# One pool of 13 SBUF buffers for attention's features and the feed-forward tiles, and a new order of the steps

## The chip, the cores and the metric

The kernel runs on one core of one Trainium2 chip. The metric is the time of one execution in device microseconds (us). The engines are TensorE (PE in the profile, its weight loads PEld), VectorE (DVE), ScalarE (ACT), GpSimd (POOL) and SyncE (SP), which issues the DMA transfers here. Each engine takes its instructions in the order in which the program has them, and waits on semaphores for the others.

## What is computed

```python
def phi(x):                                   # q, k: (8, 8, 576, 64), w_phi: (64, 128)
    proj = np.einsum('bhsd,df->bhsf', x, w_phi)
    proj = proj - np.max(np.abs(proj), axis=-1, keepdims=True)
    return np.concatenate([np.exp(proj), np.exp(-proj)], axis=-1)
q_p, k_p = (phi(q), phi(k))
kv = np.einsum('bhsf,bhsd->bhfd', k_p, v)
z = np.sum(k_p, axis=2)
num = np.einsum('bhsf,bhfd->bhsd', q_p, kv)
den = np.einsum('bhsf,bhf->bhs', q_p, z)[..., None] + 1e-06
x = ((num / den).transpose(0, 2, 1, 3)).reshape(4608, 512)
h = x @ w_in                                  # w_in: (512, 1024)
e = np.exp(h - np.max(h, axis=-1, keepdims=True))
solu = h * (e / (np.sum(e, axis=-1, keepdims=True) + 1e-09))
ln = (solu - mean(solu)) / np.sqrt(var(solu) + 1e-06) * g_ln
out = ln @ w_out                              # w_out: (1024, 512)
```

## The kernel before

**Two halves.** Attention is cut into 16 units (8 batches, two groups of four heads each), each with two pairs of heads, called sub 0 and sub 1 here. The feed-forward half is cut into 36 tiles of 128 tokens; nine tiles cover two batches, so a tile can begin when the units of its batches have been divided. The program runs the units and, from the third unit on, the tiles between them.

**A unit.** SP loads q, k and v. PE projects them (`pjq`, `pjk`, and `pjm` for the middle part). DVE takes the maximum and subtracts it (`m`, `dq`, `dk`), ACT takes the exponentials into the features `fq` and `ek`. PE sums keys times values and the keys into `kvT`: the step K (from `ek` and `rawv`), a rest (from `ek` and `vz`) and the step Z, the sum of the keys (from `zacc` and `ones`). DVE turns `kvT` into `kvs` (step kve), one DMA writes it out (`dk<-kvs`, kvo) and a second brings it back in another shape (`kvf<-dk`, kvi). PE then makes `num` and `den` from `fq` and `kvf`; a part of the numerator (step qr) has the output `kvT`. ACT takes `den` to `dn`, DVE inverts it to `cmr`, a DMA writes it (`d<-cmr`), another spreads it over the partitions (`rb<-d`), and POOL multiplies it into the rows of x (`xa`, `xb<-E,rb`).

**A tile.** ACT and POOL split x into a high and a low part (`mxh`, `mxl`). PE makes `h` in 24 matmuls of 512 columns: `win_h` with `mxh`, `win_l` with `mxh`, `win_h` with `mxl`. DVE finds the maximum (`nm`), ACT the exponential (`eu`), DVE the product with h, its statistics (`bst`, `mv`) and a transposed copy (`ub`); two DMAs turn it round (`du<-ub`, `uTs<-du`); ACT and POOL split it again (`uhs`, `uls`), PE makes `o` in 24 matmuls, ACT scales it into `os`, and a DMA writes `out`.

**What sets the order.** The program is a list of 2457 steps. `SEQUENCE` (lines 54 to 184) is a table of their numbers: `order()` (line 229) walks it, and its order is the order of the instructions on every engine. The same walk gives out the SBUF buffers: every tag has a list of free buffers (`SBUF_BUFS`, line 45); a step that needs one takes the first of the list, and a buffer goes back to its end when the last step that reads it has been passed.

**Tags.** `e` has 6 buffers of 4608 bytes per partition, for attention's features `ek` and `fq` and the `eu` of the last tiles. `big` has 8 of 4096 bytes, for the other tiles' `eu`, `ub`, `uTs`, `uhs` and `uls`, and at the start for the weights while they are split.

```python
            for tag, t in o["alloc"]:
                slot[t] = free[tag].pop(0)
            for t in tiles[i]:
                pending[t] -= 1
                if not pending[t]:
                    free[tag_of[t]].append(slot[t])
```

Every instruction is issued through one helper line, so all of them stand under line 260 in the profile, and are told apart by the names of their tiles.

Of the kernel before, what the change touches and what calls it, by code (L numbers as in the profile page):

```python
# [45 lines left out]
    rk=4, rkm=2, rv=3, m=8, d=3, e=6, eh=2, za=2, kf=2, q5=3, pm=1, E=2, dE=2, rb=2, G=1,  # L46
    vz=2, xa=1, xb=1, m2k=5, big=8, nm=2, sm=3, bst=2, mv=2, sa=2, sc=3,
)
SIZES = dict(
    big=4096, e=4608, q5=5120, rk=2048, rv=2048, d=2048, eh=2048, za=2048, m2k=2048, pm=1024, kf=1536, rkm=512, vz=512,  # L50
# [144 lines left out]
def pool(n):  # L195
    return 2.05 * n + 250
# [75 lines left out]
def linear_attention_then_moe(ctx, tc, qT, kT, v, w_phi, w_in, g_ln, w_out, out):  # L272
# [150 lines left out]
    op("warm", "tensor", WARM * 430, -1e4, warm_up, (), (), [("a", "warm")])  # L423
    op("gain", "sync", (475, 450), 5, g_load)
    raw_tag = ("xb", "xa", "xb", "xa")
    w_tag = ("big",) * 8
    w_time = W_TIME
    w_mean_at = W_MEAN
    for i in range(8):
# [877 lines left out]
```

## Time and profile before

| what | us |
|---|---|
| median of 3 runs | 663.02 (662.71 to 663.58) |
| the profiled execution | 664.01 |
| its span, first to last instruction | 662.20 |
| PE busy in the span | 653.7 |
| POOL, DVE, ACT busy | 409.1, 495.1, 368.9 |

The profiled execution has 1.81 us outside its span, and is 0.99 us above the median. TensorE's granted clock is 1.00 in every slice of the span. A row of a timeline begins with its start and its length; several instructions of one kind in a row are put together, with their count behind an x, and the bracket at its end names the time that the engine stood idle before and what ended it.

### The profile page before, as it was taken

The numbers are of one execution on the slowest core, as the hardware profiler recorded it, in microseconds if no ns is written. First come the engines' busy times: TensorE is split into PE (matmuls) and PEld (weight loads), VectorE is DVE, ScalarE is ACT, GpSimd is POOL, SyncE is SP. The second block draws the span as 40 slices with busy tenths as digits, with TensorE's granted clock in tenths as the row PEclk, the third lists the DMA queues.
The fourth block names the chain that finished last, engine by engine and source line by source line (L and its number), as shares of the span: only waits on it lengthen the run. The fifth ranks groups of instructions, "written<-read, shape, count | busy, mean of one in ns | idle before, by whom it ended". The sixth has DMA issues, their size and how long they took to land.

```text
span 662.2 us, 13124 instructions
## 1 busy us (share of the span) xinstructions
PE 653.7 (99%) x4900; PEld 490.5 (74%) x4900; DVE 495.1 (75%) x750; ACT 368.9 (56%) x713; POOL 409.1 (62%) x447
## 2 busy tenths in 40 slices
PE   8999999999999999999999999999999999999997
PEld 6766767668777777777777777877677877788886
DVE  6999987788978687799968879788679665355340
ACT  4997775466564744556565665355745464324221
POOL 0239998757866546667876575856654775455342
PEclk9999999999999999999999999999999999999999
DMA  8987787887487946887667856874786544424241
GB/s 269 346 270 237 221 251 210 270 259 214 134 265 255 296 151 182 272 260 230 201 197 230 287 151 176 266 227 124 229 282 199 191 149 120 123 110 162 112 167 72
DMA packets 133296, 138.45 MB, mean 209 GB/s; under 512 B 55664, under 2 KB 106736, under 8 KB 132720
## 3 DMA queue, kind: packets, MB, share of 16 engines
q1 hardware_dynamic: 133232, 137.61, 65.9%
q8 instruction: 39, 0.64, 0.4%
q14 instruction: 25, 0.20, 0.1%
HBM read 87.10 MB, written 50.48 MB: 208 GB/s over the span
## 4 chain that ended last, share of the span: by engine, by line
PE 87%; DVE 6%; DMA 4%; issue 1%; ACT 1%; SPq 0%; ACTq 0%
PE o L260 30%; PE h L260 29%; PE kvT L260 11%; PE num L260 6%; PE pjk L260 4%; PE pjq L260 4%; PE den L260 2%; DVE m L260 2%; DVE w L260 1%; DVE dq L260 1%; DMA rawq<-in_q 1%; DVE dk L260 1%; DMA pT<-dqd 1%; PE pjm L260 1%; DMA dk<-kvs 1%
## 5 line engine op out<-in xcount | busy, mean ns | idle before, releaser
L260 POOL TENSOR_TENSOR uls<-uTs,uhs 128x1024 fp32r<-128x1024 f32 x36 | 86.6, 2410 | 61.8 <-ACT uhs L260 47.6
L260 PE MATMUL o<-w_out_h,uhs 128*128 128x512 f32 (+1 forms) x296 | 114.6, 387 | 0.0
L260 ACT ACTIVATE ek<-dk 128x512 f32<-128x512 f32 (+1 forms) x160 | 89.7, 584 | 44.1 <-DVE dk L260 39.4
L260 PE MATMUL o<-w_out_l,uhs 128*128 128x512 f32 (+1 forms) x296 | 113.6, 384 | 0.0
L260 PE MATMUL o<-w_out_h,uls 128*128 128x512 f32 (+1 forms) x296 | 113.5, 383 | 0.0
L260 PE MATMUL h<-win_h,mxh 128*128 128x512 f32 x288 | 91.2, 398 | 0.3 <-DVE dq L260 0.3
L260 DVE TENSOR_REDUCE nm<-h 128x1 f32<-128x1024 f32 x36 | 43.9, 1218 | 62.9 <-PE h L260 62.9
L260 PE MATMUL h<-win_l,mxh 128*128 128x512 f32 x288 | 88.9, 390 | 0.0
L260 PE MATMUL h<-win_h,mxl 128*128 128x512 f32 x288 | 88.8, 389 | 0.0
L260 ACT ACTIVATE fq<-pT 128x512 f32<-128x512 f32 (+1 forms) x140 | 74.5, 559 | 21.4 <-DMA pT<-dqd 13.8
L260 POOL TENSOR_TENSOR zt<-ek 128x512 f32<-128x512 f32 x52 | 68.8, 1322 | 24.4 <-ACT ek L260 22.8
L260 ACT ACTIVATE eu<-h,nm 128x1024 f32<-128x1024 f32 x36 | 40.0, 1111 | 69.3 <-DVE nm L260 60.3
L260 PEld LDWEIGHTS o<-w_out_h,uhs 128*128 128x128 f32 x296 | 55.6, 188 | 13.4 <-issue 1.6
L260 PEld LDWEIGHTS o<-w_out_h,uls 128*128 128x128 f32 x296 | 55.6, 188 | 11.0
L260 PEld LDWEIGHTS o<-w_out_l,uhs 128*128 128x128 f32 x296 | 55.6, 188 | 10.6
L260 PEld LDWEIGHTS h<-win_h,mxh 128*128 128x128 f32 x288 | 52.4, 188 | 13.9 <-issue 1.1
L260 PEld LDWEIGHTS h<-win_l,mxh 128*128 128x128 f32 x288 | 54.0, 188 | 11.5
L260 PEld LDWEIGHTS h<-win_h,mxl 128*128 128x128 f32 x288 | 54.1, 188 | 11.5
L260 PE MATMUL kvT<-ek,rawv 128*64 128x256 f32 x512 | 61.9, 384 | 0.0
L260 POOL TENSOR_TENSOR xa<-E,rb 128x576 f32<-128x576 f32 (+1 forms) x32 | 29.7, 931 | 51.9 <-DMA rb<-d 40.7
L260 DVE TENSOR_TENSOR eu<-h,eu 128x1024 f32<-128x1024 f32 x36 | 43.6, 1212 | 17.9 <-ACT eu L260 17.7
L260 PE MATMUL num<-fq,kvf 128*64 128x448 f32 (+1 forms) x304 | 56.2, 500 | 0.0
(96 smaller groups left out, 1231.9 us busy)
## 6 DMA issues: line engine op xcount, KB each, us to landing
du<-ub SPq DMA_DIRECT2D x36, 512.0 KB, 3.7
uTs<-du SPq DMA_DIRECT2D x36, 512.0 KB, 4.9
rb<-d SPq DMA_DIRECT2D x64, 144.0 KB, 4.4
dqd<-dq SPq DMA_DIRECT2D x14, 640.0 KB, 4.3
pT<-dqd SPq DMA_DIRECT2D x14, 640.0 KB, 5.8
out<-os SPq DMA_DIRECT2D x35, 256.0 KB, 3.2
rawq<-in_q SPq DMA_DIRECT2D x32, 256.0 KB, 4.7
rawk<-in_k SPq DMA_DIRECT2D x32, 256.0 KB, 4.5
```

The source lines that it names most:

```text
L260: return self.tc.keep_in_program_order(method(*args, **kwargs))
```

## The change

The tag `big` is gone; `e` has 13 buffers of 4608 bytes, and everything that used `big` takes `e`. That is 59,904 bytes per partition in place of 60,416. The table `SEQUENCE` is a new one in all its 128 lines. No step is added, removed or changed in what it computes.

```diff
-    rk=4, rkm=2, rv=3, m=8, d=3, e=6, eh=2, za=2, kf=2, q5=3, pm=1, E=2, dE=2, rb=2, G=1,
-    vz=2, xa=1, xb=1, m2k=5, big=8, nm=2, sm=3, bst=2, mv=2, sa=2, sc=3,
+    rk=4, rkm=2, rv=3, m=8, d=3, e=13, eh=2, za=2, kf=2, q5=3, pm=1, E=2, dE=2, rb=2, G=1,
+    vz=2, xa=1, xb=1, m2k=5, nm=2, sm=3, bst=2, mv=2, sa=2, sc=3,
...
-    2, 123, 1, 124, 125, 78, 127, 126, 313, 94, 87, 85, 129, 80, 81, 95, 128, 82, 83, 99, 96, 84, 98, 136, 97,
...
+    123, 2, 1, 78, 124, 125, 80, 127, 126, 128, 83, 135, 85, 79, 94, 87, 81, 95, 89, 136, 84, 141, 138, 104, 82,
...
-    w_tag = ("big",) * 8
+    w_tag = ("e",) * 8
...
-        M["uh", t] = sb("big", [P, 8, P], F32R, "uhs")
+        M["uh", t] = sb("e", [P, 8, P], F32R, "uhs")
...
-        M["ul", t] = sb("big", [P, 8, P], F32R, "uls")
+        M["ul", t] = sb("e", [P, 8, P], F32R, "uls")
...
-        e_tag = "e" if tail(t) else "big"
+        e_tag = "e"
...
-            tg = "q5" if t >= TURN_Q else "big"
+            tg = "q5" if t >= TURN_Q else "e"
```

Three places show what the new table does. In the rows, a name stands for the tiles above, and x counts equal instructions in a row.

First, DVE just ahead of the first tile, some 5 us before the first `h`: the subtractions into `dq`, of which the last frees the PSUM bank that `h` takes. Before:

```order
L260 TENSOR_REDUCE m<-pjq 128x4
L260 TENSOR_REDUCE m<-pjk 128x4
L260 STREAM_TRANSPOSE kvs<-kvT 128x3x4x32
L260 TENSOR_TENSOR dq<-pjq,m 128x4x4x32
L260 TENSOR_TENSOR dk<-pjk,m 128x512
L260 TENSOR_TENSOR dk<-pjm,m 128x128
L260 TENSOR_TENSOR dq<-pjq,m 128x4x4x32 x2
```

After:

```order
L260 STREAM_TRANSPOSE kvs<-kvT 128x3x4x32
L260 TENSOR_REDUCE m<-pjq 128x4
L260 TENSOR_REDUCE m<-pjk 128x4
L260 TENSOR_REDUCE m<-pjq 128x4
L260 TENSOR_TENSOR dk<-pjk,m 128x512
L260 TENSOR_TENSOR dq<-pjq,m 128x4x4x32 x2
```

The order among these few is another one, and the same steps stand ahead of the last pair of `dq`, counted from the start of the program: 105 steps with 109 instructions on DVE, 62 steps on PE and 13 on POOL (ahead of the first `mxl`).

Second, PE at the fourth unit's first pair, whose Z (`kvT<-zacc,ones`) stands near the third unit's second `den`. Before:

```order
L260 MATMUL kvT<-ek,rawv 64x256 x8
L260 MATMUL kvT<-fq,kvf 64x128 x4
L260 MATMUL num<-fq,kvf 64x448 x4
L260 MATMUL kvT<-ek,vz 64x256 x4
L260 MATMUL den<-fq,kvf 32x288 x8
L260 MATMUL kvT<-zacc,ones 32x128 x4
L260 MATMUL h<-win_h,mxh 128x512 x2
```

After:

```order
L260 MATMUL kvT<-ek,rawv 64x256 x8
L260 MATMUL num<-fq,kvf 64x448 x4
L260 MATMUL kvT<-fq,kvf 64x128 x4
L260 MATMUL kvT<-ek,vz 64x256 x4
L260 MATMUL kvT<-zacc,ones 32x128 x4
L260 MATMUL den<-fq,kvf 32x288 x8
L260 MATMUL h<-win_h,mxh 128x512 x2
```

Z has moved ahead of the `den`, and on DVE its kve has moved ahead of the turn of tile 2 (`ub<-eu`).

Third, PE at the last `den` of all, that of the sixteenth unit's second pair, for which tile 31 waits. Before, with the first of the 24 matmuls of tile 26's `o` behind it (the `h` of tile 27 and the `o` of tile 28 follow, 24 matmuls each, and then the `h` of tile 31):

```order
L260 MATMUL num<-fq,kvf 64x288 x8
L260 MATMUL num<-fq,kvf 64x448 x4
L260 MATMUL den<-qz,ones 32x288 x4
L260 MATMUL o<-w_out_h,uhs 128x512
L260 MATMUL o<-w_out_l,uhs 128x512
```

After, with the end of tile 28's `o` ahead and the beginning of tile 27's `h` behind (the `o` of tile 26 follows, and then the `h` of tile 31):

```order
L260 MATMUL o<-w_out_l,uhs 128x512
L260 MATMUL o<-w_out_h,uls 128x512
L260 MATMUL den<-qz,ones 32x288 x4
L260 MATMUL num<-fq,kvf 64x288 x8
L260 MATMUL h<-win_h,mxh 128x512 x2
L260 MATMUL h<-win_l,mxh 128x512 x2
```

A `num` has moved from ahead of the `den` to behind it, and the 24 matmuls of one tile's `o` from behind it to ahead of it.

## Rows read from the trace of the kernel before

**Rows 1.** The page, part 1: busy us, share of the span, instructions.
```profile
PE 653.7 (99%) x4900; PEld 490.5 (74%) x4900; DVE 495.1 (75%) x750; ACT 368.9 (56%) x713; POOL 409.1 (62%) x447
```

**Rows 2.** Busy time of each engine in three stretches of the span.
```profile
core 0: us, PE busy (x) PEld busy (x) DVE busy (x) ACT busy (x) POOL busy (x), PEclk, DMA share, GB/s
5.10:67.10 62.00, 59.33 (x824) 42.14 (x823) 61.68 (x110) 50.88 (x98) 26.10 (x16) 1.00 0.89 290
45.40:104.80 59.40, 57.69 (x598) 39.06 (x596) 55.21 (x93) 44.02 (x91) 58.34 (x47) 1.00 0.79 244
...
105.00:655.00 550.00, 550.00 (x3726) 416.31 (x3723) 399.62 (x586) 288.97 (x555) 344.75 (x386) 1.00 0.64 200
```

**Rows 3.** Waits of PE: us in total, times, longest.
```profile
PE kvT L260 <- DMA kvf<-dk: 1.3, 1, 1.3
PE pjm L260 <- DMA rawk<-in_k: 0.9, 2, 0.6
...
PE h L260 <- DVE dq L260: 0.3, 1, 0.3
```

**Rows 4.** Timelines, 0 to 7 and 64 to 70 us: start, length, instruction.
```profile
5.13 1.29 DVE L260 TENSOR_REDUCE m<-pjq 128x4 f32<-128x512 f32 x2 [5.13 <-PE pjq L260]
...
65.68 1.27 DVE L260 TENSOR_TENSOR dq<-pjq,m 128x512 f32<-128x512 f32 x2
...
66.27 1.26 POOL L260 TENSOR_TENSOR mxl<-xa,mxh 128x512 fp32r<-128x512 f32 x1
...
67.10 0.70 PE L260 MATMUL h<-win_h,mxh 128*128 128x512 f32 x2 [0.30 <-DVE dq L260]
...
68.10 0.63 PE L260 MATMUL h<-win_h,mxl 128*128 128x512 f32 x2
```

**Rows 5.** Timeline of PE and of DVE, 87 to 101 us.
```profile
88.00 1.18 PE L260 MATMUL den<-fq,kvf 128*32 128x288 f32 x16
89.00 0.40 PE L260 MATMUL kvT<-zacc,ones 128*32 128x128 f32 x8
...
96.54 1.95 PE L260 MATMUL kvT<-ek,rawv 128*64 128x256 f32 x16
99.79 0.66 PE L260 MATMUL kvT<-fq,kvf 128*64 128x128 f32 x8 [1.31 <-DMA kvf<-dk]
...
89.54 0.58 DVE L260 STREAM_TRANSPOSE kvs<-kvT 128x384 f32<-128x384 f32 x1 [0.73 <-ACT E L260]
```

**Rows 6.** The chain of work that ended last: start, length, step.
```profile
90.15 5.31 DMA dk<-kvs
95.48 4.27 DMA kvf<-dk
...
260.67 1.50 PE num L260 x8
...
266.03 2.95 PE o L260 x12
268.98 2.72 PE h L260 x12
...
561.21 3.59 PE num L260 x24
...
630.93 27.55 PE o L260 x144
```

**Rows 7.** Timeline at the last den, and at the last tile's split.
```profile
564.73 0.69 PE L260 MATMUL den<-qz,ones 128*32 128x288 f32 x8
...
575.80 0.32 POOL L260 TENSOR_TENSOR xa<-E,rb 128x64 f32<-128x64 f32 x1 [5.33 <-DMA rb<-d]
...
577.83 1.12 ACT L260 ACTIVATE eu<-h,nm 128x1024 f32<-128x1024 f32 x1 [8.15 <-DVE nm L260]
...
580.20 1.29 POOL L260 TENSOR_TENSOR mxl<-xa,mxh 128x512 fp32r<-128x512 f32 x1 [2.83 <-ACT mxh L260]
...
645.81 2.40 POOL L260 TENSOR_TENSOR uls<-uTs,uhs 128x1024 fp32r<-128x1024 f32 x1 [2.53 <-ACT uhs L260]
```

More of the change, by code (lines that the diff above doesn't have):

```diff
@@ L45 @@
 SBUF_BUFS = dict(
-    rk=4, rkm=2, rv=3, m=8, d=3, e=6, eh=2, za=2, kf=2, q5=3, pm=1, E=2, dE=2, rb=2, G=1,
-    vz=2, xa=1, xb=1, m2k=5, big=8, nm=2, sm=3, bst=2, mv=2, sa=2, sc=3,
+    rk=4, rkm=2, rv=3, m=8, d=3, e=13, eh=2, za=2, kf=2, q5=3, pm=1, E=2, dE=2, rb=2, G=1,
+    vz=2, xa=1, xb=1, m2k=5, nm=2, sm=3, bst=2, mv=2, sa=2, sc=3,
 )
 SIZES = dict(
-    big=4096, e=4608, q5=5120, rk=2048, rv=2048, d=2048, eh=2048, za=2048, m2k=2048, pm=1024, kf=1536, rkm=512, vz=512,
+    e=4608, q5=5120, rk=2048, rv=2048, d=2048, eh=2048, za=2048, m2k=2048, pm=1024, kf=1536, rkm=512, vz=512,
     xa=10240, xb=8192, E=2304, rb=2304, dE=1152,
@@ L1156, in moe_uh @@
         if i == 0:
-            M["uh", t] = sb("big", [P, 8, P], F32R, "uh")
-            M["ul", t] = sb("big", [P, 8, P], F32R, "ul")
+            M["uh", t] = sb("e", [P, 8, P], F32R, "uh")
+            M["ul", t] = sb("e", [P, 8, P], F32R, "ul")
         nc.scalar.copy(out=M["uh", t][:, 4 * i : 4 * i + 4, :], in_=M["uT", t, i])
@@ L1235, in linear_attention_then_moe @@
             op(n("uh", 0), "scalar", act(DF), z + 11, moe_uhs, (t,), [n("bi")],
-               [("big", n("uh"))], [n("uT")])
-            op(n("ul", 0), "gpsimd", pool(DF) + 25, z + 12, moe_uls, (t,), [n("uh", 0)], [("big", n("ul"))], [n("uT"), n("uh")])
+               [("e", n("uh"))], [n("uT")])
+            op(n("ul", 0), "gpsimd", pool(DF) + 25, z + 12, moe_uls, (t,), [n("uh", 0)], [("e", n("ul"))], [n("uT"), n("uh")])
         for i in range(0 if by_dma else 2):
@@ L1241, in linear_attention_then_moe @@
             op(n("uh", i), "scalar", act(512, True), z + 10.5 + i, moe_uh, (t, i), [n("t", i)] + ([n("uh", 0)] if i else []),
-               () if i else [("big", n("uh")), ("big", n("ul"))], [n("uT", i), n("uh")])
+               () if i else [("e", n("uh")), ("e", n("ul"))], [n("uT", i), n("uh")])
             op(n("ul", i), "vector", dve(512), z + 11 + i, moe_ul, (t, i), [n("uh", i)], (),
```

254 rows, old and new, of the table SEQUENCE are left out of this document.

## The prediction

> **What bounds the kernel now.** I read the page's busy shares first. PE is busy for 653.7 us of the 662.20 us span, 99% [rows 1], so at most 8.5 us of it are not matmuls, whatever the order does. The busy time by stretch says where these are: from 105 to 655 us PE is busy for 550.00 of 550.00 us [rows 2]. In that stretch no step waits for a buffer, a transfer or another engine in a way that costs time, so an order that makes waits shorter there wins nothing; it can only lose. What can be won lies before 105 us, and there the waits of PE name it [rows 3]: one wait of 1.3 us for `kvf<-dk`, 0.9 us for loads of `rawk`, 0.3 us for DVE's `dq` ahead of the first `h`, and a few as small.
>
> These waits are not worth the same. Up to the first `h` at 67.10 us [rows 4] the end is set by DVE, not by PE: from 5.10 to 67.10 us DVE is busy for 61.68 us of 62.00 [rows 2], from its first `m` at 5.13 to the pair of `dq` that ends at 65.68 + 1.27 = 66.95 us, and `h` starts 0.15 us later, its wait ended by that `dq` [rows 4]. PE's waits for the loads of `rawk` all lie ahead of this point, under DVE's work. The wait for `kvf<-dk`, at 99.79 us [rows 5], lies behind it, where PE sets the end.
>
> **The change, part by part.** No instruction is added or removed, so the work of each engine is what it was: the sum is made of waits, and of what PE loses between matmuls of unlike shapes.
>
> *The buffers.* One list of 13 in place of lists of 6 and 8. A wait for a buffer that this takes away would have to be seen in the trace of before, and none of PE's waits is ended by the reader of an `e` or `big` tile: they end with transfers and with DVE [rows 3]. So the gain is 0. That is a statement on before; what the shared list may cost is a rival below.
>
> *Up to the first `h`.* The same 105 steps stand on DVE ahead of the pair of `dq`, in another order. DVE has 0.32 us of idle time there [rows 2] and cannot begin before the first projection. Its 61.68 us of work fit into no less, so the first `h` starts between 66.8 and 67.1 us, if DVE stays as full. I take no change, and 0.3 us as the most to win. POOL's `mxl` for the same tile ends at 66.27 + 1.26 = 67.53 us, and `h` takes it first at 68.10 [rows 4]; 13 steps stand ahead of it on POOL in both programs, and POOL is busy for 58.34 of the 59.40 us around it [rows 2], so it moves no more than DVE does. The loads that are moved on SP, and the moved `cmall` on PE, are covered by the same DVE work; were that cover gone, waits like PE's 0.9 us for `rawk` [rows 3] would be what they cost.
>
> *The wait at 99.79 us.* This is the only one behind the first `h`. Read backwards [rows 5, 6]: the matmul waits for `kvf<-dk`, 95.48 + 4.27 = 99.75; that for `dk<-kvs`, 90.15 + 5.31 = 95.46; that for DVE's `kvs`, 89.54 + 0.58 = 90.12; and that for Z on PE, which runs from 89.00 for 0.40 us, right behind a `den` that takes 89.00 - 88.00 = 1.00 us. The new order puts Z ahead of this `den`, and on DVE `kvs` ahead of the turn of tile 2. So the chain starts 1.00 us earlier. What stands on PE between Z and the waiting matmul gains the `den` and loses nothing, so the point at which PE needs `kvf` stays. Of 1.31 us, 0.31 are left: **-1.00 us**. The bounds: all of it (-1.31), if the write takes 4.27 us, as the read does, and not 5.31; nothing (0), if DVE is late with `kvs` by as much as PE is early, since other work stands ahead of it on DVE too (0.73 us of idle time before `kvs` here speak against that [rows 5]).
>
> *Shapes.* On PE the order of attention's small matmuls among the large ones is new. Counted in the two programs, the stretches of one tile shape become 231 in place of 224; of the changes of shape behind the first `h` there are 186 in place of 184, and the others lie under DVE's time. The chain gives a price: the first 12 matmuls of an `o` behind projections take 2.95 us, the next 12 take 2.72 [rows 6], so 0.23 us for one change. Two more: **+0.46 us**. The bounds are 0, since a part of such a change may be the last small matmul's own end, and 7 x 0.23 = 1.6 us, if those ahead of the first `h` are not hidden.
>
> The Trainium skill, TensorEngine Tiling (Array Packing), section Key Properties, speaks against the change here: it says that changing the tiling mode drains the TensorE. By that rule each of the 7 changes would cost its drain wherever it stands, and with the 0.23 us of the row the sum would be 1.1 us higher; the trace bears the drain out by that row, and DVE's 61.68 of 62.00 us against its counting ahead of the first `h`.
>
> *The end.* Behind the last `h` PE runs without a break, 27.55 us of `o` [rows 6]. In both programs seven half tiles of `o` (seven times 2.72 us) stand between the last `h` and the last tile's own `o`, and the order of the last output is the same. The last split `uls` ends at 645.81 + 2.40 = 648.21 us [rows 7], where PE needs it at 630.93 + 7 x 2.72 = 649.97 us; the new order begins that tile's turn on DVE no later. So 0.
>
> The sum, against the profiled execution: 662.20 - 1.00 + 0.46 = 661.66 us of span. Its 1.81 us outside the span stay; but it ran 0.99 us above the median of the runs, so the median is its span and 0.82 us: 661.66 + 0.82 = 662.48, say **662.5 us**, 0.5 us (0.08%) below the median. About 0.2%, 1.33 us, is what a measurement of this kernel can tell from no change, so this counts as no change.
>
> **The rivals.**
>
> *Slower: tile 31 comes too early.* Behind the last `den` the path to tile 31's x goes through ACT, DVE, two DMAs, POOL, ACT and POOL. In before it ran from 564.73 + 0.69 = 565.42 us to the end of `mxl` at 580.20 + 1.29 = 581.49 us [rows 7], 16.07 us, and PE had three times 5.44 us to do, with 0.23 for a change of shape some 16.5 us, and did not wait. In the new order a `num` and two groups of 24 stand there: 3.59 - 1.50 = 2.09 us [rows 6], twice 5.44, and 0.23: 13.2 us. `h` takes `mxl` 68.10 - 67.10 = 1.00 us behind its start [rows 4], so PE can do without it for 14.2 us. If the path is as long as before, PE waits 16.07 - 14.2 = 1.9 us: 662.48 + 1.9 = **664.4 us**. It is slower by over 0.2% from a path of 16.1 us on (1.87 us above the sum), and a little less if the gain of 1.00 us is lost too. For it: SP has two transfers of tile 30 ahead of `d<-cmr`, and POOL the `uls` of tile 30 (2.40 us for its like [rows 7]) ahead of the last multiplication. Against it: in before a part of the path was ACT's order. `rb` was there at 575.80 us, the two multiplications (0.32 and some 1.3 us) end at 577.4, but ACT split x only behind an `eu` that started at 577.83 and waited for DVE and PE [rows 7]; without it `mxl` could end at 577.4 + 0.6 + 1.3 = 579.3, 13.9 us behind the `den`. In the new order the `h` in question comes 5.4 us earlier.
>
> *Slower: the shared list.* A tile's `eu`, `ub`, `uTs`, `uhs` or `uls` now takes a buffer that attention's matmuls free, or the other way round. Followed through the two tables, 55 buffers go from a tile to attention's features and 68 from them to a tile; before it is 13, all of the weights, at the start. Where the reader stands late on PE, POOL's or SP's instruction waits, and all that stands behind it on its queue. The tightest place that I find by laying before's durations under the new order is the `uls` of tile 18 near 444 us, whose buffer is freed by a K of the fourteenth unit some 0.6 us before it must start. One instruction of 2.40 us [rows 7] in its way makes it 2.40 - 0.6 = 1.8 us late: **664.3 us**. Against it: PE needs nothing of 550 us sooner than it has it [rows 2], so there is room of some us nearly everywhere.
>
> *Faster: all waits go.* The whole 1.31 us, the 0.30 us ahead of the first `h`, and no price for shapes: 662.20 - 1.61 + 0.82 = **661.4 us**. It needs three bounds at once. The Trainium skill, Perfetto Trace Analysis, section Optimization Strategy, says that bubbles that repeat can mean too few buffers for the next tile, and by it a larger pool would win more; the trace shows no gap that repeats on PE from 105 us on (550.00 of 550.00 us).
>
> *The change does not do what it says* would be a list of 13 that leaves every wait where it is: 663.0 to 663.5 us, no change either, and within the forecast's own range.
>
> **How the numbers follow.** The forecast's own range, 661.7 to 664.3 us, no change: 0.60, with the change that does nothing in it. Tile 31: 0.15. The shared list: 0.13. All waits go: 0.12. So faster 0.12, same 0.60, slower 0.28. The range is from 661.3 (all waits go, with 0.1 us for the spread of the runs) to 665.8: the sum, with the gain of 1.31 us turned into none and tile 31's wait on top (662.48 + 1.31 + 1.9 = 665.7). Beyond it are both slower rivals at once, some 1 in 10, and little on the other side.
>
> **What would show it.** In the trace of after: the first `h` at 66.8 to 67.1 us behind a `dq`; DVE busy for all but some 0.3 us before it; Z some 1 us earlier against the first `h`, and a wait for `kvf` of 0 to 0.5 us near 99 us; PE busy for 550 of 550 us from 105 us on; no wait at tile 31's `h`, near 580 us, for `mxl`; 27.5 us of `o` at the end. What would make the prediction wrong: DVE idle for over 1 us before the first `h` (the new order starves it), or a wait of PE behind 105 us that ends with POOL's `mxl` or `uls`.

## The result and the profile after

| | median, us | runs |
|---|---|---|
| before | 663.11 | 662.71 to 663.58 (4 runs) |
| after | 667.29 | 665.88 to 667.97 (4 runs) |

The ratio is 1.0055 (95% interval 1.0043 to 1.0066): the new kernel is 0.55% slower, some 3.6 to 4.2 us. The prediction was 662.5 us, with a range of 661.3 to 665.8 and a chance of 0.28 for slower. The profiled execution of after took 667.97 us, with a span of 666.1 us against 662.2.

The busy times of the engines in the stretches of [rows 2], now of after (columns: stretch and length, then busy us and instructions of PE, PEld, DVE, ACT, POOL, the granted clock, the share of the DMA engines, GB/s):

```profile
5.10:67.10 62.00, 59.70 (x824) 42.39 (x822) 60.17 (x107) 49.77 (x98) 22.11 (x15) 1.00 0.87 284
...
105.00:655.00 550.00, 548.16 (x3705) 413.80 (x3702) 396.37 (x589) 286.83 (x552) 349.55 (x390) 1.00 0.64 199
```

Both lines differ from what the argument stood on. DVE is busy for 60.17 us of the first 62 us, not 61.68, so it idles for 1.83 us, the time up to its first instruction at 5.78 us included; and PE is no longer busy for all of the 550 us. The first of the two does not mark the new order by itself: a second profile of before, reported below, has 60.52 us there. The waits of PE in after, which answer to [rows 3] (us in total, times, longest):

```profile
PE dT L260 <- DVE dq L260: 1.2, 1, 1.2
PE h L260 <- POOL mxl L260: 1.0, 2, 0.7
...
PE pjm L260 <- ACT cms L260: 0.7, 1, 0.7
PE den L260 <- DVE dq L260: 0.7, 1, 0.7
PE pjq L260 <- DMA rawq<-in_q: 0.4, 1, 0.4
PE o L260 <- POOL uls L260: 0.4, 1, 0.4
```

The wait for `kvf` of [rows 3] is gone, and new ones stand there that end with POOL's `mxl` and `uls`. Two of them lie behind 105 us (`uls` at 112 us, `mxl` at 326 us): what the prediction named as the sign that it is wrong.

**Where the time went.** Since PE does the same steps in both kernels, the start of one step in one trace, less its start in the first trace of before, says how far PE is behind at that point. The table has this difference in us for a second execution of before, three of after, and two kernels of the experiments. "Tile 18's h" lies behind a `den` near 391 us that is spoken of below.

| step (its start in the first trace of before) | before, 2nd | after, 1st | after, 2nd | after, 3rd | before's order, one list | after, both edits |
|---|---|---|---|---|---|---|
| first h, tile 0 (67.10) | 1.18 | 1.52 | 1.16 | 1.24 | 0.05 | 1.77 |
| h of tile 2 (77.93) | 1.18 | 2.13 | 1.34 | 1.86 | 0.05 | 1.80 |
| h of tile 3 (105.19) | -0.34 | 0.65 | -0.19 | 0.33 | -1.48 | 0.48 |
| second half of tile 2's o (113.56) | -0.38 | 1.25 | 0.05 | 0.77 | -1.19 | 1.08 |
| second half of tile 4's o (196.43) | -0.38 | 1.35 | 0.10 | 0.86 | -0.75 | 1.17 |
| h of tile 10 (205.44) | -0.38 | 2.77 | 0.10 | 2.04 | -0.74 | 1.17 |
| h of tile 20 (351.97) | -0.37 | 3.84 | 0.90 | 3.04 | -0.73 | 1.29 |
| h of tile 18 (393.98) | -0.39 | 3.97 | 1.03 | 3.17 | 0.31 | 1.42 |
| h of tile 35 (625.33) | -0.39 | 3.96 | 1.03 | 3.17 | 0.33 | 1.44 |

Read downwards, a jump in a column is time lost or won between two points. It can be larger than the one wait that is named for it: in the first trace of after PE loses 1.42 us up to tile 10's `h`, and the `den` that waits there stood idle for 0.66 us; the rest is lost at the matmuls beside it. All jumps come before 400 us. From there to the end no column moves by more than 0.1 us.

### The profile page after: what moved, and what is told of

Same layout as the page of the kernel before. It is cut to its first block, busy times and chain, and to the rows that moved or that the text cites. A ratio compares the mean times of both kernels' runs of the same rounds, so it can differ in the third digit from the quotient of the medians.

```text
span 666.1 us, 13109 instructions
## 1 busy us (share of the span) xinstructions
PE 656.5 (99%) x4900; PEld 492.3 (74%) x4900; DVE 490.5 (74%) x750; ACT 367.4 (55%) x713; POOL 408.5 (61%) x447
## 4 chain that ended last, share of the span: by engine, by line
PE 74%; DMA 5%; POOL 5%; ACT 2%; DVE 1%; issue 1%; SPq 0%; POOLq 0%; ACTq 0%; DVEq 0%
PE o L260 27%; PE h L260 25%; PE kvT L260 9%; PE num L260 5%; PE pjk L260 3%; PE pjq L260 2%; PE den L260 2%; DMA rb<-d 1%; POOL w_out_l L260 1%; DMA pT<-dqd 1%; POOL zacc L260 1%; DMA dk<-kvs 1%; DMA d<-cmr 1%; POOL zt L260 1%; DMA dqd<-dq 1%
## 5 line engine op out<-in xcount | busy, mean ns | idle before, releaser
L260 DVE SCALAR_TENSOR_TENSOR qz<-fq,kvf,qz 128x576 f32<-128x576 f32 x46 | 45.2, 999 | 20.7 <-ACT qz L260 15.3
L260 ACT ACTIVATE qz<-fq,kvf 128x576 f32<-128x576 f32 x46 | 34.5, 768 | 43.5 <-DMA kvf<-dk 43.5
L260 POOL TENSOR_TENSOR xa<-E,rb 128x576 f32<-128x576 f32 (+1 forms) x32 | 27.9, 873 | 49.0 <-DMA rb<-d 46.2
```

Of the source, the lines that this page charges most:

```text
L260: return self.tc.keep_in_program_order(method(*args, **kwargs))
```

## The experiments

The names of the steps are those of the kernel's description; units are counted from one, as there. "Theory" letters are those of the expectations.

### The list alone

The table of before, with the tags of after:

```diff
-    d=3, e=6, ..., big=8, ...
+    d=3, e=13, ...
```

> The table of before with the one list of 13 buffers: the pool alone, without the new order. Theory A (the time was lost to the order of the steps: transfers held up in SP's queue and steps put too near to those they wait for): within 0.7 us of before, 662.4 to 663.8, no wait of PE behind 105 us, first h at 67.1 us. Theory B (it was lost to the shared list: instructions wait for buffers whose last readers stand late on another engine): slower than before by 1.5 us or more, 664.6 and up, with waits on PE behind 105 us.

Measured: 665.37 us against 663.55, ratio 1.0021 (1.0009 to 1.0034). Theory A's range fell: the list costs some 0.2% in the old order too. Its medians lie 1.82 us apart, which is B's 1.5 us or more; by the ratio it is 1.4 us (0.6 to 2.3), which leaves B open. The first `h` came at 67.14 us, as A says, and the trace has waits behind 105 us, as B says: 0.44 us are lost at tile 4's `o` and 1.06 us at a `den` near 391 us (in the table's column "before's order, one list"). Around the second one (timeline; the bracket is the idle time before and what ended it):

```profile
386.07 1.11 ACT L255 ACTIVATE eu<-h,nm 128x1024 f32<-128x1024 f32 x1 [2.13 <-PE o L255]
...
387.18 0.76 ACT L255 ACTIVATE qz<-fq,kvf 128x576 f32<-128x576 f32 x1
387.31 1.22 DVE L255 TENSOR_TENSOR eu<-h,eu 128x1024 f32<-128x1024 f32 x1 [1.34 <-ACT eu L255]
388.20 2.37 POOL L255 TENSOR_TENSOR uls<-uTs,uhs 128x1024 fp32r<-128x1024 f32 x1 [0.71 <-PE kvT L255]
388.45 2.73 DVE L255 SCALAR_TENSOR_TENSOR qz<-fq,kvf,qz 128x576 f32<-128x576 f32 x1
...
391.24 0.69 PE L255 MATMUL den<-qz,ones 128*32 128x288 f32 x6 [0.40 <-DVE qz L255]
```

ACT stands 2.13 us at tile 17's `eu`, until a matmul of `o` ends: by the hand-out of the list this `eu` gets the buffer of tile 15's `uhs`, whose last reader that `o` is. ACT's `qz` is behind it, and DVE's `qz` behind the product with this `eu`; it then meets a POOL split and takes 2.73 us, and the `den` waits.

### The same, with one chain taken out of the way

First ACT's part alone was moved:

```diff
 ACT:  ... 
+      qz (twelfth unit, second part)
       eu (tile 17)
-      qz (twelfth unit, second part)
```

> The table of before with the one list of 13, and one step moved: ACT's second part of the twelfth unit's qz ahead of tile 17's eu, which waits 2.1 us for a buffer that tile 15's o frees. Theory P (the shared list costs where an instruction waits for a buffer and the next on its queue is urgent): the 0.6 us wait of a den near 391 us goes, PE's position at tile 18's h is 0.9 to 1.1 us better than with the list alone, 664.3 us against 665.4. Rival (the den is late by DVE or by another way): no change there.

Measured: 665.38 us, ratio 1.0032 (1.0018 to 1.0047), and the `den`'s step is 1.06 us longer as before. The expectation fell; DVE's order had been left as it was. Then DVE's part was moved as well:

```diff
 DVE:  qz (twelfth unit, first part)
+      qz (twelfth unit, second part)
       product with eu (tile 17)
-      qz (twelfth unit, second part)
```

> The table of before with the one list of 13, and two steps moved: ACT's and DVE's second part of the twelfth unit's qz both ahead of tile 17's eu and its product, on their engines. In the first try only ACT's part was moved; DVE's qz still stood behind the product of that eu, ran beside a POOL split and took 2.72 us, and the den kept its wait of 0.8 us. Theory P (the list makes eu wait for the buffer that tile 15's o frees, and the queue behind it is late): qz runs at 386 us or before in 0.8 to 1.2 us, the den near 391 us does not wait, PE's way from that den to the next step is 1.06 us shorter in the trace; 664.3 us against 665.4. Rival: the den waits as before.

Measured: 664.70 us, ratio 1.0019 (1.0010 to 1.0029). In its trace both parts of `qz` run in one piece and the `den` goes through without a wait:

```profile
385.79 1.60 DVE L255 SCALAR_TENSOR_TENSOR qz<-fq,kvf,qz 128x576 f32<-128x576 f32 x2
...
390.80 0.67 PE L255 MATMUL den<-qz,ones 128*32 128x288 f32 x8
```

The step that was 1.06 us longer in both traces of this order with the wait is as short as in the three traces with two lists. The chain is shown. What it is worth in the time is not: the medians moved by 0.7 us, within what they scatter, and the ratio to before by nothing (1.0021 with the list alone, 1.0019 here). The other loss, at tile 4's `o` (0.33 to 0.44 us in all three traces with the list, none in the three without), was not taken apart, and it is less than the 0.2% that the list costs; where the rest of that comes from stays open.

### The second and third profile of the two kernels

> The kernel before, unchanged, profiled a second time. The prediction took 1.0 us off for a wait of PE of 1.3 us at 99.8 us, from one profiled execution that was 1.0 us above the median. Theory V (that wait is an accident of that execution: the same order with the list of 13 did not have it): no wait for kvf near 99 us, h of tile 3 at 103.7 us and not at 105.2 us. Rival (the wait belongs to the order): again 1 us or more there.

> The new kernel, unchanged, profiled a second time, to tell which of its waits belong to its order. Theory S: rb<-d again issued near 59.4 us, the first h again at 68.4 us or later and waiting for mxl; the waits at 205 us (1.4 us) and at 325 us (0.8 us) again there, within 0.3 us. Rival V (they vary like those of the start): one of the two gone.

> The new kernel, unchanged, profiled a third time, to tell waits of its order from accidents. Theory: 0.7 to 1.0 us at tile 15's h again; first h at 68.0 us or later again; each of the waits at 112 us (uls), 205 us (den) and 305 us (h of tile 13) there or not there, as in the profiles so far. Rival: the wait at tile 15's h is gone, or the first h is at 67.3 us or before.

Before took 663.62 us in this run, and its trace has no wait for `kvf`. Chain and matmul, to be held against [rows 5] and [rows 6] (a row of SP's queue is the issue of a transfer):

```profile
90.72 0.58 DVE L260 STREAM_TRANSPOSE kvs<-kvT 128x384 f32<-128x384 f32 x1 [0.73 <-PE kvT L260]
91.33 0.33 SPq L260 DMA_DIRECT2D dk<-kvs  x1
94.43 0.60 SPq L260 DMA_DIRECT2D kvf<-dk  x1
...
99.50 0.61 PE L260 MATMUL kvT<-fq,kvf 128*64 128x128 f32 x8
```

`kvf<-dk` is issued 3.1 us behind `dk<-kvs`, not 5.3 as in the first profile, and takes some 3.0 us, not 4.3; the matmul finds its data. Why these transfers were slower in the first profile stays open. Theory V holds: the wait of 1.31 us belonged to that one execution, which was also 0.99 us above its median. The first `h` came at 68.28 us, 1.18 us late, with the order of before. DVE stood there for the transfer that frees its buffer:

```profile
66.84 1.29 DVE L260 TENSOR_TENSOR dq<-pjq,m 128x512 f32<-128x512 f32 x2 [1.14 <-DMA dqd<-dq]
```

After took 664.96 and 667.09 us. In both, tile 15's `h` waits as in the first. The loss at 205 us is there in the third and not in the second: of these two waits, one belongs to the order, and one comes and goes.

### The prediction's gain by itself

On PE the fourth unit's Z ahead of the third unit's `den`, in the table of before, with two lists:

```diff
 PE:   kvT<-ek,vz
+      kvT<-zacc,ones
       den<-fq,kvf
-      kvT<-zacc,ones
 DVE:
+      kvs<-kvT
       ub<-eu (tile 2)
-      kvs<-kvT
```

> The kernel before with one change of order: the fourth unit's Z ahead of the third unit's second den on PE, and its kve ahead of the turn of tile 2 on DVE. The prediction's term by itself: the chain to kvf starts 1.0 us earlier, the wait of PE at 99.8 us falls from 1.3 to 0.3 us, 662.0 us (661.6 to 662.4). Rival (the chain is set by the DMA queues or by DVE, not by Z): the wait stays at 1.3 us, 663.0 us.

Measured: 663.41 us against 663.55, ratio 0.9997 (0.9983 to 1.0011): no difference. The wait is not in its trace, and it is not in the second trace of before either. There was nothing to win.

### The start in before's order

The first 420 steps of the new table sorted as before has them; in the second kernel SP's steps alone:

```diff
-SEQUENCE = new[:420] + new[420:]
+SEQUENCE = (new[:420] in the order of before) + new[420:]
```

> The new kernel, with the first 420 of its steps (to tile 2's h, 83 us) in the order in which before has them; the rest of the new table and the list of 13 stay. Theory A: the first h comes back from 68.6 to 67.1 us and its mxl is in time, so 2.1 us are won: 665.2 us (664.8 to 665.9, if part of it goes into a longer wait for tile 2's uls), span 664.0. The waits near 205 and 325 us stay. Theory B: the start holds no buffers that have passed from a tile to attention, so nothing changes: 667 us.

> The new kernel, with SP's transfers alone, among the first 420 steps, in the order in which before has them; the other four engines keep the new order. Theory A1 (in the first 67 us SP's queue is what holds up: a dqd<-dq and the rb<-d behind a wait for d<-cmr): the first h comes at 67.1 to 67.5 us, 1.5 to 2.1 us are won, 665.2 to 665.8 us. Theory A2 (the new order of DVE and POOL is what is late, as the split of the third block of w_in behind the last multiplication on POOL): less than 0.5 us won, 666.8 us or more, first h at 68 us or later.

Measured: 667.53 us, ratio 1.0059 (1.0034 to 1.0083), and 676.71 us, 1.0191 (1.0163 to 1.0219). Of the waits of PE, two rows of the first and one of the second:

```profile
PE o L255 <- POOL uls L255: 1.0, 1, 1.0
...
PE kvT L255 <- ACT fq L255: 0.8, 1, 0.8
```

```profile
PE pjm L255 <- DMA rawk<-in_k: 4.5, 1, 4.5
```

The first brought `h` to 67.68 us and tile 2 to 0.84 us behind, so it won 0.5 to 1.3 us there against the three profiles of after; by the second half of tile 2's `o` it was 1.87 us behind, more than after itself in any of its three profiles. What was won came back at tile 2's `uls` and at a `kvT` that waits for `fq` (at 100 us). The second lost 10 us at the start: with the other four engines in the new order, the loads in the old order come too late. PE has nothing to do from 34 to 37 us, and behind this its granted clock is 0.50, the lower of its two levels (1.2 GHz in place of 2.4), from 40 to 46 us. Theory A1 fell in this form; it tells nothing of the new order's own loads, only that one engine's order cannot be exchanged alone.

### Four transfers, then the same with one put back

In the new order SP's queue near 54 us, of after (timeline):

```profile
53.64 0.33 SPq L260 DMA_DIRECT2D d<-cmr  x1
...
59.44 0.58 SPq L260 DMA_DIRECT2D rb<-d  x1
...
62.70 0.43 SPq L260 DMA_DIRECT2D dqd<-dq  x1
```

The `rb<-d` needs the `d<-cmr` to have landed. From issue to landing (transfers issued between 53 and 60 us: size, median us), in after and then in before:

```profile
d<-cmr SPq DMA_DIRECT2D x1, 4.5 KB, 5.7
```

```profile
d<-cmr SPq DMA_DIRECT2D x1, 4.5 KB, 2.6
```

Until that `rb<-d` can be issued, all that stands behind it on SP waits, the `dqd<-dq` of 62.70 among it (before issued it at 59.77 us). Three rows of after show what follows on POOL, DVE and PE:

```profile
65.09 1.40 POOL L260 TENSOR_TENSOR xa<-E,rb 128x576 f32<-128x576 f32 x1 [3.61 <-DMA rb<-d]
...
67.27 1.29 DVE L260 TENSOR_TENSOR dq<-pjq,m 128x512 f32<-128x512 f32 x2 [1.12 <-DMA dqd<-dq]
...
70.11 0.73 PE L260 MATMUL h<-win_h,mxl 128*128 128x512 f32 x2 [0.30 <-POOL mxl L260]
```

The edit, as the second try has it. In the first try the third unit's `dqd<-dq` stood ahead of the two `rb<-d`, and the load marked ! behind that of `rawk`; the second put this load back:

```diff
 SP:   d<-cmr (second unit, second pair)
       rb<-d (its first pair)
!      rawv<-in_v (third unit)
+      rb<-d, rb<-d (its second pair)
+      dqd<-dq (third unit, 640 KB), dqd<-dq (fourth unit)
       rawk<-in_k (fifth unit)
-      rb<-d, rb<-d, dqd<-dq further down, dqd<-dq further up
```

> The new kernel with four transfers moved on SP's queue, all before 67 us: dqd<-dq of the third unit (640 KB) behind the second d<-cmr of the second unit, the two rb<-d that wait for this d<-cmr right behind it, and dqd<-dq of the fourth unit ahead of the next loads. Theory S (d<-cmr takes 5.7 us to land in the new order because it was issued behind 640 KB and other loads, 2.6 us in before; SP stands 3.4 us at the rb<-d behind it, and this holds up the first mxl, and through the second dqd<-dq the DVE): rb<-d is issued near 56.5 us and not at 59.4, the first h starts at 67.1 to 67.6 us in place of 68.6 and does not wait for mxl; 2 us won by 89 us; of it 0.5 to 1.5 us are given back near 112 us, where uls of tile 2 waits on POOL behind a multiplication. 665.5 to 667 us. Rival (DVE's own new order is what is late): first h at 68.3 us or later.

> The new kernel with SP's transfers near 54 us in another order: behind the second unit's second d<-cmr first the load of v that the next K needs, then the two rb<-d that wait for the d<-cmr, and only then the third unit's dqd<-dq (640 KB), the fourth's dqd<-dq and the load of k. In the first try the load of v was moved back as well, and PE waited 2.9 us for it. Theory S: rb<-d is issued by 57 us, no wait of PE for v, first h at 67.1 to 67.6 us, no wait for mxl: 1.5 to 2.1 us won by 89 us and 0.5 to 1.2 of it given back at tile 2's uls (POOL is full there); 666.0 to 666.8 us. Rival (DVE or POOL set the first h in the new order): no better than 68.3 us.

The first: 667.96 us, ratio 1.0059 (1.0041 to 1.0076); the wait for `mxl` is gone, and PE stands for `rawv`:

```profile
PE kvT L255 <- DMA rawv<-in_v: 2.9, 1, 2.9
```

The second: 666.59 us, ratio 1.0057 (1.0038 to 1.0076). The `rb<-d` is issued at 56.05 us. In this kernel, and in the one with both edits below, DVE does not wait for `dqd<-dq`, and PE loses only 0.06 and 0.03 us between tile 0's `h` and tile 2's, where it loses 0.10 to 0.68 us in the five traces that have the new order there. So the chain from `d<-cmr` is shown. Yet the first `h` came at 68.05 and 68.87 us and not at 67.1 to 67.6; here the expectation fell. DVE's rows tell why. From its first `m` to the pair of `dq` it has the same 109 instructions; they take 61.5 to 61.6 us in the six traces that start in before's order, and 62.4 and 62.7 us in these two. One instruction has most of it, a split of a weight (the second try, then before):

```profile
61.62 2.31 DVE L255 SCALAR_TENSOR_TENSOR w<-wraw,w 128x1024 uint32<-128x1024 uint32 x1
```

```profile
61.46 1.23 DVE L260 SCALAR_TENSOR_TENSOR w<-wraw,w 128x1024 uint32<-128x1024 uint32 x1
```

Beside it runs POOL's multiplication `xa<-E,rb`, from 61.00 to 62.86 us, which the earlier `rb<-d` let begin; the kernel with both edits has the same 2.31 us. The edit took a wait away and put a collision of DVE and POOL in its place. No median gain can be told.

### The middle

Three waits behind 105 us, one edit for each; and these with the first edit of the start:

```diff
 POOL: uls (tile 2)
       xa, xb<-E,rb (third unit, first pair)      was ahead of it
 PE:   pjk (eighth unit, last part)               was behind the den
       num, kvT, den (seventh unit)
 SP:   rb<-d (ninth unit, second pair)
       uTs<-du (tile 9)                           was ahead of it
```

> The new kernel with three steps moved, one at each wait of PE behind 105 us: POOL's multiplication of the third unit behind uls of tile 2 (112 us); the projection of the eighth unit's last part (1.1 us of PE) ahead of the seventh unit's num, which waits for kvf (205 us); SP's uTs<-du of tile 9, which waits 2.0 us for a buffer that an o frees, behind the rb<-d of the ninth unit that stood behind it (325 us). Theory S: 0.4 us won at 112 us, 1.0 to 1.4 at 205, 0.8 at 325; 2.3 us in all, 665.0 us (664.5 to 665.6), and the start as in the new kernel. Rival (the chains behind are as long, so each wait turns up at the next step): PE's position at tile 20's h still 3.5 us or more behind that of before, 667 us.

> The edits of the two kernels above together. Theory S: PE stands 0.3 to 0.8 us ahead of the kernel before from 105 us on, the wait for tile 2's uls is gone, span 661.5 to 662.3, 662.5 to 663.6 us: what the prediction's sum gave. Rival (the waits move on): 665 us or more.

Measured: 673.90 us, ratio 1.0137 (1.0103 to 1.0171), and 675.16 us, 1.0143 (1.0101 to 1.0185). Two of the three edits made new waits (waits of PE in the first of the two kernels):

```profile
PE pjk L255 <- DVE dq L255: 3.8, 1, 3.8
...
PE o L255 <- ACT E L255: 1.4, 1, 1.4
```

The projection that was put ahead takes a PSUM bank that a `dq` frees later, 3.8 us; and the `o` of tile 2 takes one that ACT frees behind the multiplication that was moved, 1.4 us. The projection's move cost more than its wait: PE loses 6.43 us between the second half of tile 4's `o` and tile 10's `h`. Behind the 3.78 us in which it stood, its granted clock is 0.84 from 206 to 209 us and 0.59 from 209 to 212, and the eight matmuls of `num` take 2.92 us there, 1.72 in after, where the clock is 1.00. In the second kernel the wait is 3.3 us and the granted clock 0.73, 0.50 and 0.63 in the stretches from 206 to 215 us. So these two times do not tell what the other edits would be worth without that wait. The third edit did what it should: from 292 to 352 us PE loses nothing (-0.18 us), where after loses 0.80. It was kept, and the second replaced by a step on DVE:

```diff
 SP:   rb<-d (ninth unit, second pair)
       uTs<-du (tile 9)                           was ahead of it
 DVE:
+      dq (ninth unit)
       qz, qz (seventh unit, second and first part)
-      dq (ninth unit)
```

> The new kernel with two steps moved: SP's uTs<-du of tile 9, which waits for a buffer that an o frees, behind the rb<-d of the ninth unit; and on DVE a subtraction of the ninth unit (dq, whose bank the seventh unit's den takes) ahead of that unit's second qz, which waits for ACT. Theory S: the 0.8 us at 325 us go, as in the earlier run, and 0.6 of the 1.4 us at 205 us; 666.0 us (1.4 us better than the new kernel), PE at tile 20's h 2.2 to 2.6 us behind before if the start is as in the new kernel. Rival: the den waits for qz just as long, 0.8 us won.

> The new kernel with the edits of the second tries at the start and in the middle together (the order of SP's transfers near 54 us; uTs<-du of tile 9 behind the rb<-d; a dq of the ninth unit ahead of the seventh unit's qz). Theory S+P: no wait for mxl in tile 0 beyond 0.2 us, none at tile 15's h (0.85 us in the five profiles without the edit), none at 205 us; 665.2 us (664.6 to 665.9), so 1 to 2 us better than the new kernel and still above before, since the first h stays near 68 us. Rival (the waits move on to other steps): 666.5 us or more.

Measured: 666.21 us, ratio 1.0047 (1.0031 to 1.0063), and with the second edit of the start 665.74 us, 1.0039 (1.0027 to 1.0052). Tile 15's `h` does not wait in either, while PE loses 0.7 to 1.0 us there in all seven profiles whose order has the transfer ahead. After, and then the kernel with both edits:

```profile
316.79 0.37 SPq L260 DMA_DIRECT2D uTs<-du  x1
317.22 0.58 SPq L260 DMA_DIRECT2D rb<-d  x1
...
322.92 1.41 POOL L260 TENSOR_TENSOR xa<-E,rb 128x576 f32<-128x576 f32 x1 [1.73 <-DMA rb<-d]
324.29 1.27 POOL L260 TENSOR_TENSOR mxl<-xb,mxh 128x512 fp32r<-128x512 f32 x1
...
325.62 0.73 PE L260 MATMUL h<-win_h,mxl 128*128 128x512 f32 x2 [0.68 <-POOL mxl L260]
```

```profile
313.19 0.58 SPq L255 DMA_DIRECT2D rb<-d  x1
315.16 0.37 SPq L255 DMA_DIRECT2D uTs<-du  x1
...
320.90 1.26 POOL L255 TENSOR_TENSOR mxl<-xb,mxh 128x512 fp32r<-128x512 f32 x1
...
323.15 0.62 PE L255 MATMUL h<-win_h,mxl 128*128 128x512 f32 x2
```

In after, SP had issued its last transfer at 314.76 us and stood 2.03 us at `uTs<-du` of tile 9: by the hand-out it gets the buffer of tile 6's `uls`, whose last reader, tile 6's second `o`, ends at 316.72. Behind it stood the `rb<-d` on which tile 15's x hangs. With the two the other way round the `rb<-d` goes 2 us and more earlier, and `mxl` ends before `h` takes it.

The wait at 205 us (a `den` that waits for a `dq`) is in neither, but it was also in only two of the seven profiles that have no edit there, so this tells nothing. No version beat before.

## Why the prediction was wrong, point by point

**The first `h`: the bound was read as a fact of the order.** The step said that DVE's 61.68 us of work fit into no less, so `h` comes at 66.8 to 67.1 us, "if DVE stays as full". That bounds it from below only. In six traces with before's order at the start (before twice, the two lists with Z moved, the list alone, its two edits) it came at 67.10, 68.28, 67.22, 67.14, 69.02 and 68.23 us, mean 67.8; in five with the new order there (after three times, and the two kernels that changed only the middle) at 68.62, 68.26, 68.34, 69.73 and 70.04, mean 69.0. By tile 2 the means are 0.75 and 2.34 us behind, so the new order loses some 1.6 us here, and the first trace of before was the earliest of its kind.

What fails in the step is the sentence that the loads moved on SP are covered by DVE, and with it the term of nothing. SP's queue also holds the `dqd<-dq` that frees DVE's buffer, and the `rb<-d` that the first `mxl` waits for. In all eleven traces `h` starts 0.05 to 0.15 us behind the `dq`, so DVE's row can be taken apart:

| up to the first `h`, mean us | before's order (6) | new order (5) |
|---|---|---|
| DVE's first `m` starts | 5.56 | 5.82 |
| its 109 instructions | 61.54 | 61.80 |
| its idle time between them | 0.59 | 1.33 |
| from the end of `dq` to `h` | 0.15 | 0.06 |
| first `h` | 67.83 | 69.00 |

The greatest part is idle time, and nearly all of that is the wait for `dqd<-dq`: it was over 0.15 us in three of six traces of before's order (1.14, 0.98, 0.25) and in four of five of the new one (1.12, 0.80, 1.65, 1.45), and in neither of the two with the second edit of the start. The first `m` scatters in both orders, from 5.13 to 6.13 us and from 5.30 to 6.13. The longer work is a weight's split beside POOL's `xa` in three of the five traces, `w<-wraw`, which took 1.62 to 1.80 us there and at most 1.41 in the other eight. To this come 0.4 us between tile 0's and tile 2's `h`, the wait for `mxl`. So the sign that the prediction named, DVE idle for over 1 us, came true, but it came in before's second profile too.

**The wait at 99.79 us: -1.00 us that was not there.** The term was right as to place and cause and wrong as to weight: one profile was taken for the kernel. The second profile of before and the three traces of its order with the one list do not have the wait: one in five has it. The prediction had noted that its execution ran 0.99 us above the median, and took the gain all the same. The same term is counted wrongly in the upper end of the range: it adds 1.31 us for a lost gain of which the sum had taken off 1.00, so that end is rightly 665.4 us; the result lies beyond either.

**Shapes: +0.46 us.** Between tile 3's `h` and tile 35's the second profile of after loses 1.03 + 0.19 = 1.22 us. Of it 0.73 us are tile 15's wait; 0.49 are left for all other things, tile 2's `uls` among them, so the term was not too small. The drain that the Trainium skill states (TensorEngine Tiling (Array Packing), Key Properties) shows up at no more than that here.

**Behind 105 us no wait.** This failed: PE was busy for 548.16 us and not 550. That it was busy throughout with the old order said nothing on the slack of a new one. The rival "shared list" had the mechanism (a buffer freed late by PE holds an instruction and its queue), with 0.13 and at another place: not the `uls` of tile 18, but `uTs<-du` of tile 9 on SP. Its price of 1.8 us stands against 0.7 to 1.0 measured. The rival "tile 31" did not happen, no trace has a wait there; but its chain, a late `rb<-d` and an x that comes too late, is tile 15's.

**Before had such waits too.** The number of instructions that wait for a buffer of these lists for over 0.3 us, by the hand-out laid over the traces, is 17 to 19 in before and in after, some 40 us in all in before and some 35 in after. The shared list does not make more of them. It puts them elsewhere, and what counts is what stands behind on the queue. (Of the 13 buffers that pass from one use to the other in before, eight are the weights', not all; five go from attention to the `eu` of the last tiles.)

**The sum that the runs give:** 1.6 us at the start, 0.85 at tile 15, 0.3 to 0.5 for shapes, some 0.4 for the wait at 205 us (1.2 to 1.4 in two of seven profiles), some 0.2 at tile 2's `uls`: 3.4 us, against 0.55% of 663 us, 3.6. The traces agree: at tile 35's `h` the three of after stand 2.72 us behind the first trace of before on average, and the three with two lists in before's order 0.52 us ahead of it, 3.2 us apart. The terms for shapes and for `uls` are estimates from what is left in single traces. The list by itself has 0.2% in before's order. How much of the new order's loss two lists would have spared can't be told: with it they would have to hold 8 and 8 buffers, 69,632 bytes per partition, and it wasn't tried.

## What to carry to other kernels

An engine that is busy for 99% of the span tells where a gain is not; it does not tell what a reordering may lose, and that has to be read from the slack of every transfer and buffer against the queue behind it. Before a wait of 1 us is booked as a gain, profile the kernel a second time. When instructions share one list of buffers, ask of each one that takes a buffer which reader frees it, and what stands behind it on its in-order queue: a transfer that can wait belongs behind one that can't.

## What the runs showed of the hardware

- The same DVE instruction, `qz<-fq,kvf,qz` on 128x576, takes 0.77 to 0.83 us in most of its 46 places, and up to 2.73 us where POOL runs beside it. In the row of the list alone, above, it begins at 388.45, POOL's `uls` ends at 390.57, and `qz` ends at 391.18, 0.61 us later. The Trainium skill, SBUF — State Buffer, section Who interferes with whom, says that a DVE instruction with two SBUF inputs contends with a GpSimd instruction that reads SBUF; the same page, section Summary: rules for kernel authors, says that the second one to issue blocks until the first has finished. The trace agrees with its 2.73 us beside POOL, against 0.77 to 0.83 in most places. A second case is the `w<-wraw,w` of the second edit of the start, 2.31 us beside POOL's `xa<-E,rb` and 1.23 us in before and after.
- A transfer of 4.5 KB (`d<-cmr`) took 5.7 us from issue to landing in after, where 640 KB (`dqd<-dq`) had been issued 1.6 us before it and 656 KB followed within 2.4 us, and 2.6 us in before, where that `dqd<-dq` was issued 1.2 us behind it. The other two profiles of after have 6.0 and 6.1 us, and the four kernels with an edit of the start, which issue the `dqd<-dq` behind it, 2.7 to 3.8 us.
- The start varies by 1 to 2 us from execution to execution: the first `h` came at 67.10 and 68.28 us in two executions of before, and between 67.10 and 69.02 us in the six traces that have its order there.
- After a wait of 3.78 us TensorE's granted clock went from 1.00 to 0.84 and 0.59 in the next two stretches of 3 us, and the eight `num` matmuls took 2.92 us in place of 1.72.
